# Attention in 64-token steps of two batches, in 64x64 quarters of the array, with transposed outputs

## The chip, the cores and the metric

The kernel runs on one NeuronCore of a Trainium2 chip. The metric is the device time of one execution in microseconds. Engine names are those of the profile: PE is the matrix engine (PEld its weight loads), DVE the vector engine, ACT the scalar engine, POOL the GpSimd engine, SP the engine that issues most DMAs here.

## The reference

The reference is a gated linear attention followed by a feed-forward layer. With 4 batches, 8 heads, 768 tokens and a head size of 48:

```python
for t in range(S):
    state = alpha[:, :, t, :, None] * state + np.einsum('bhd,bhe->bhde', k[:, :, t], v[:, :, t])
    y[:, :, t] = np.einsum('bhd,bhde->bhe', q[:, :, t], state)
x = y.transpose(0, 2, 1, 3).reshape(B * S, H * D)        # 3072 x 384
h = x @ w_in                                             # 384 -> 2048
sp = np.maximum(h, 0.0) + np.log1p(np.exp(-np.abs(h)))
out = (h * erf(sp)) @ w_out                              # 2048 -> 384
```

## The kernel before

Attention goes in 24 chunks of 128 tokens of one batch, six in a row for each batch. The steps of a chunk are methods of `Chunk`:

- `ld` issues seven DMAs on SP's queue (alpha, k and q in two halves each, v once) into one set of raw tiles. Heads go in pairs: partitions 0 to 47 hold the dimensions of the even head of a pair, 64 to 111 those of the odd one, with the 128 tokens along the free axis. `a0` counts entries of alpha above a limit.
- `a1` forms the running product A of alpha along the tokens, one scan of 128 elements for each of the four pairs.
- `a2` and `a3` form 1/A (by Ln, Exp and a correction step on DVE), the scaled keys K = k/A and the scaled queries Q = q*A.
- `a4` multiplies K and Q of each head to the 128x128 scores pS, masks them into sT (one DVE operation for the even heads, one for the odd ones), and transposes K to pn, copied to kn.
- `a5` forms the outputs py, with tokens on the partitions: Q times the state T, plus masked scores times v. They are copied to y by ACT. Then pu = kn times v updates the state T (four DVE operations on 64 partitions each; in the first chunk of a batch two).
- `a6` transposes y on PE (px) and splits it into two float32r parts, x_hi (ACT) and x_lo (DVE), each 384 columns for the chunk.

Two chunks make a block of 256 tokens, whose feed-forward layer is `Moe`. `H` multiplies x by w_in (tile ph; three products for each pair of parts, f32r, 144 matmuls of 256 columns a block), `L1`, `L2`, `E` and `Z` are the activation on ACT and DVE, and `O` multiplies by w_out (tile acc, 96 matmuls of 384 columns a block).

The order in which steps are given out is written by hand in the tables `START`, `ORDER` and `TAIL`; within it a scheduler orders each engine's instructions. `START` also loads and splits the weights, `ORDER` is repeated for the blocks in between. `a5_0` there is the second chunk of the next block, `a5_1` the first of the one after that:

```python
"... Z_2@-1 ld_1 a5_0 a6_0 H_0_0@1 H_0_1@1 L2_0 L2_1 O_2_0@-1 O_2_1@-1 "
"O_3_0@-1 L1_2 L2_2 a1_1 a2_1 a3_1 a4_1 O_3_1@-1 L1_3 L2_3 a5_1 a6_1 ld_2 out@-1 "
```

If values leave the range that this way can carry, `general` computes everything anew; with these inputs it does not run.

Of the kernel before, what the change touches and what calls it, by code (L numbers as in the profile page):

```python
# [14 lines left out]
AMIN = 1e-18  # L15
# [5 lines left out]
AHI = 1.3  # L21
# [5 lines left out]
# The order in which the steps of chunks (128 tokens) and blocks (256) are given out: the start with the weights, the  # L27
# same for each block in between, and the end.
# [21 lines left out]
def gla_moe(ctx: ExitStack, tc: tile.TileContext, q, k, v, alpha, w_in, w_out, out):  # L50
    nc = tc.nc
    B, CPB, _, D, NP, P = q.shape
    H, S = 2 * NP, CPB * P
# [25 lines left out]
    for nm, fill in (("a", 1.0), ("q", 0.0), ("k", 0.0)):  # L79
        t = raw.tile([P, NP, P], F32, name=f"raw_{nm}")  # L80
        nc.vector.memset(t, fill)
        raws.append(t)
# [3 lines left out]
    maskn = const.tile([P, P], F32, name="maskn")  # L86
    nc.gpsimd.memset(maskn, -1.0)
    nc.gpsimd.affine_select(
        out=maskn, in_=maskn, pattern=[[1, P]], compare_op=ALU.is_ge, fill=0.0, base=0, channel_multiplier=-1
    )  # L90
# [4 lines left out]
    flags = const.tile([P, B * CPB, 2], F32, name="flags")  # L95
# [3 lines left out]
    nc.gpsimd.memset(hflags, 0.0)  # L99

# [20 lines left out]
    state = {"T": at.tile([P, NP, 2, D], F32, name="T", tag="T", bufs=1)}  # L121
    nc.gpsimd.memset(state["T"], 0.0)

    class Chunk:
        def __init__(self, n):
            self.n = n
            self.first = n % CPB == 0
            self.last = n % CPB == CPB - 1

        def ld(self):  # L130
            b, c = divmod(self.n, CPB)
            self.ra, self.rq, self.rk = raws
            self.vt = raw.tile([P, H, D], F32, name="raw_v", tag="raw_v")
            for t, src in ((self.ra, alpha), (self.rk, k), (self.rq, q)):
                for par in range(2):
                    nc.sync.dma_start(out=t[par * HD : par * HD + D], in_=src[b, c, par])
            nc.sync.dma_start(out=self.vt, in_=v[b, c])

        def a0(self):
            junk = at.tile([P, NP, P], F32, name="junk", tag="w", bufs=1)  # L140
            nc.scalar.activation(junk, self.ra, AF.Relu, bias=bhi, accum_out=flags[:, self.n, 1:2])

        def a1(self):
            self.A = at.tile([P, NP, P], F32, name="A", tag="A", bufs=1)
            for pair in range(NP):
                nc.vector.tensor_tensor_scan(  # L146
                    out=self.A[:, pair, :], data0=self.ra[:, pair, :], data1=floor.broadcast_to([P, P]), initial=1.0,
                    op0=ALU.mult, op1=ALU.max,
                )
            self.ae = at.tile([P, NP], F32, name="ae", tag="ae")  # L150
            nc.gpsimd.tensor_copy(out=self.ae, in_=self.A[:, :, P - 1])

        def a2(self):
            r = ps_at.tile([P, NP, P], F32, name="r", tag="at")
            tab(nc.scalar.activation(r, self.A, AF.Ln))
            tab(nc.scalar.activation(r, r, AF.Exp, scale=-1.0, accum_out=flags[:, self.n, 0:1]))
            w = at.tile([P, NP, P], F32, name="w", tag="w", bufs=1)
            nc.vector.tensor_tensor(out=w, in0=self.A, in1=r, op=ALU.mult)
            nc.vector.scalar_tensor_tensor(out=w, in0=w, scalar=2.0, in1=r, op0=ALU.subtract, op1=ALU.mult)
            self.w = w  # L160

        def a3(self):
            self.K = at.tile([P, NP, P], F32, name="K", tag="K")
            nc.vector.tensor_tensor(out=self.K, in0=self.rk, in1=self.w, op=ALU.mult)
            self.Q = at.tile([P, NP, P], F32, name="Q", tag="Q")
            nc.vector.tensor_tensor(out=self.Q, in0=self.rq, in1=self.A, op=ALU.mult)

        def a4(self):
            self.sT = []
            pss = [ps_at.tile([P, NP, P], F32, name="pS", tag="at") for _ in range(2)]  # L170
            for pair in range(NP):
                for par in range(2):
                    rows = slice(par * HD, par * HD + D)
                    nc.tensor.matmul(  # L174
                        out=pss[par][:, pair, :], lhsT=self.K[rows, pair, :], rhs=self.Q[rows, pair, :],
                        start=True, stop=True,
                    )
            for ps in pss:
                st = at.tile([P, NP, P], F32, name="sT", tag="sT")
                nc.vector.tensor_tensor(  # L180
                    out=st, in0=ps, in1=maskn.unsqueeze(1).broadcast_to([P, NP, P]), op=ALU.mult
                )
                self.sT.append(st)
            if not self.last:
                pn = ps_at.tile([P, NP, P], F32, name="pn", tag="at")
                for pair in range(NP):
                    nc.tensor.transpose(pn[:, pair, :], self.K[:, pair, :], ident)  # L187
                self.kn = at.tile([P, NP, 2, HD], F32, name="kn", tag="kn", bufs=1)
                nc.scalar.activation(
                    self.kn.rearrange("p a b d -> p (a b d)"), pn.rearrange("p a t -> p (a t)"), AF.Copy  # L190
                )

        def a5(self):
            vt, T = self.vt, state["T"]
            self.yt = at.tile([P, NP, 2, D], F32, name="y", tag="y", bufs=1)
            py = ps_at.tile([P, 512], F32, name="py", tag="at")
            for pair in range(NP):
                if not self.first:
                    nc.tensor.matmul(  # L199
                        out=py[:, 2 * pair * D : 2 * (pair + 1) * D], lhsT=self.Q[:, pair, :],  # L200
                        rhs=T[:, pair, :, :].rearrange("p b d -> p (b d)"), start=True, stop=False,
                    )
                for par in range(2):
                    h = 2 * pair + par
                    nc.tensor.matmul(  # L205
                        out=py[:, h * D : (h + 1) * D], lhsT=self.sT[par][:, pair, :], rhs=vt[:, h, :],
                        start=self.first, stop=self.first or par == 1,
                    )
            nc.scalar.activation(self.yt.rearrange("p a b d -> p (a b d)"), py[:, : H * D], AF.Copy)
            if not self.last:  # L210
                pu = ps_at.tile([P, 512], F32, name="pu", tag="at")
                for pair in range(NP):
                    for par in range(2):
                        nc.tensor.matmul(  # L214
                            out=pu[par * HD : (par + 1) * HD, pair * D : (pair + 1) * D],
                            lhsT=self.kn[:, pair, par, :], rhs=vt[:, 2 * pair + par, :], start=True, stop=True,
                        )
                U = pu[:, : NP * D].rearrange("p (a d) -> p a d", a=NP)
                aeb = self.ae.unsqueeze(2).broadcast_to([P, NP, D])
                for par in range(2):  # L220
                    rows = slice(par * HD, (par + 1) * HD)
                    Tp, Up, ap = T[rows, :, par, :], U[rows], aeb[rows]
                    if self.first:
                        nc.vector.scalar_tensor_tensor(
                            out=Tp, in0=Up, scalar=-1.0, in1=ap, op0=ALU.mult, op1=ALU.mult
                        )
                    else:
                        nc.vector.tensor_tensor(out=Tp, in0=Tp, in1=Up, op=ALU.subtract)
                        nc.vector.tensor_tensor(out=Tp, in0=Tp, in1=ap, op=ALU.mult)

        def a6(self, moe):
            if self.n % 2 == 0:
                moe.alloc_x()
            moe.turn(self.yt.rearrange("p a b d -> p (a b d)"), self.n % 2, ps_at, "at")
# [3 lines left out]
    class Moe:  # L238
        def __init__(self, tok, pl):
            self.tok, self.pl = tok, pl  # L240
# [6 lines left out]

        def turn(self, y, c, pool, tag):
            """Writes the 128 tokens of y, transposed, to the block's x as two parts."""
            x_hi, x_lo = self.x  # L250
            cs = slice(c * P, (c + 1) * P)
            px = pool.tile([P, 512], F32, name="px", tag=tag)
# [6 lines left out]
        def H(self, g, half):  # L259
# [21 lines left out]
            else:  # L281
                n = (self.tok // TB * NG + g) * 2 + half
# [53 lines left out]
        def out(self):  # L336
            for tt in range(2):
                o = self.pl.gp.tile([P, DM], F32, name="o", tag="o", bufs=1)
                nc.scalar.activation(o, self.acc[tt][:, :DM], AF.Copy, scale=-RT2)
                nc.sync.dma_start(out=out[bass.ds(self.tok + tt * P, P), :], in_=o)  # L340
# [5 lines left out]
    def weight(hi, lo, src, n, pool, tag):  # L346
        """Loads a matrix of float32, or of float64 as pairs of int32, and splits it into two parts."""
# [195 lines left out]
```

## Time and profile before

| what | value |
|---|---|
| runs (three) | 597.25, 598.33, 598.65 us; median 598.33 |
| profiled execution, span from first to last instruction | 594.3 us |
| PE busy | 552.4 us (93%) |
| DVE busy | 503.0 us (85%) |
| ACT busy | 485.1 us (82%) |
| POOL busy | 20.9 us (4%) |
| DMA | 36.98 MB, mean 62 GB/s |
| mean granted PE clock | 0.984 of full speed |

For the profiled execution the profile gives the span alone; the time of a run is taken around it. Matmuls are pipelined, so the records of PE overlap, and a busy PE is not a PE at its peak. The chain of waits, followed back from the last instruction, is PE for 81% of the span, DVE for 9% and ACT for 6%.

### The profile page before, as it was taken

The page shows a single profiled execution, that of the slowest core. Times are in us where ns is not written, and L with a number is a line of the kernel's source. Part 1 is how long each engine was busy: PE and PEld are TensorE (multiplying, and loading weights), DVE is VectorE, ACT ScalarE, POOL GpSimd, SP SyncE. Part 2 cuts the span into 40 slices and gives each one's busy share as a digit, 9 for nine tenths or more (in the row PEclk, how much of TensorE's full clock was granted, in tenths as well). Part 3 has the DMA queues.
Part 4 walks back from the last instruction along what each step waited for, and adds up shares of the span by engine and source line. Part 5 has one row for each costly group of instructions (what it writes and reads, how often), then busy time and mean ns, then how long its engine had stood idle before and what let it go on. Part 6 is the DMA issues. An engine that isn't in the chain of part 4 may idle for free.

```text
span 594.3 us, 11033 instructions
## 1 busy us (share of the span) xinstructions
PE 552.4 (93%) x4282; PEld 534.8 (90%) x4282; DVE 503.0 (85%) x769; ACT 485.1 (82%) x845; POOL 20.9 (4%) x40
## 2 busy tenths in 40 slices
PE   0679798999999999999999999999999999999994
PEld 0568787999999999999999999999999999999884
DVE  7899999999999869869779879879779879758780
ACT  4558979698989879889879879889788888889941
POOL 1000110002000000000000000000000000000000
PEclk9999798998999999999999999999999999999998
DMA  6584312313112102112112102112112101000001
GB/s 196 176 290 145 110 55 81 120 54 94 28 41 81 41 26 68 41 29 68 40 28 68 41 28 67 41 39 70 28 35 66 34 28 41 1 1 28 1 27 33
DMA packets 20220, 36.98 MB, mean 62 GB/s; under 512 B 3520, under 2 KB 9664, under 8 KB 20160
## 3 DMA queue, kind: packets, MB, share of 16 engines
q1 hardware_dynamic: 20160, 36.19, 19.9%
q8 instruction: 36, 0.59, 0.4%
q14 instruction: 24, 0.20, 0.1%
HBM read 31.46 MB, written 4.72 MB: 61 GB/s over the span
## 4 chain that ended last, share of the span: by engine, by line
PE 81%; DVE 9%; ACT 6%; DMA 2%; issue 1%; SPq 0%; ACTq 0%; DVEq 0%
PE acc L331 33%; PE ph L272 30%; PE py L205 7%; PE pS L174 4%; PE py L199 3%; PE pu L214 2%; DMA wst<-in_moe_w_in_dram 2%; PE pn L187 1%; PE px L254 1%; DVE hs L309 1%; DVE s L308 1%; DVE A L146 1%; ACT wbuf L360 1%; ACT w L283 1%; DVE wbuf L365 1%
## 5 line engine op out<-in xcount | busy, mean ns | idle before, releaser
L272 PE MATMUL ph<-x_hi,wi_hi 128*128 128x256 f32 x576 | 164.0, 288 | 4.0 <-ACT hs L284 3.4
L272 PE MATMUL ph<-x_lo,wi_hi 128*128 128x256 f32 x576 | 163.4, 284 | 0.4 <-DVE x_lo L257 0.4
L272 PE MATMUL ph<-x_hi,wi_lo 128*128 128x256 f32 x576 | 163.2, 284 | 0.0
L331 PE MATMUL acc<-wo_hi,gh 128*128 128x384 f32 x384 | 134.5, 351 | 3.6 <-DVE gh L320 2.6
L331 PE MATMUL acc<-wo_lo,gh 128*128 128x384 f32 x384 | 131.3, 342 | 0.0
L331 PE MATMUL acc<-wo_hi,gl 128*128 128x384 f32 x384 | 130.0, 344 | 1.2 <-DVE gl L323 1.2
L272 PEld LDWEIGHTS ph<-x_hi,wi_hi 128*128 128x128 f32 x576 | 110.4, 192 | 5.8 <-ACT hs L284 4.2
L272 PEld LDWEIGHTS ph<-x_lo,wi_hi 128*128 128x128 f32 x576 | 110.5, 192 | 0.7 <-DVE x_lo L257 0.7
L272 PEld LDWEIGHTS ph<-x_hi,wi_lo 128*128 128x128 f32 x576 | 110.5, 192 | 0.5 <-DVE wi_lo L344 0.5
L283 ACT ACTIVATE w<-ph 128x512 f32<-128x512 f32 x96 | 57.5, 599 | 46.9 <-PE ph L272 44.0
L297 DVE TENSOR_TENSOR t<-s,w 128x1024 f32<-128x1024 f32 x48 | 58.5, 1219 | 29.4 <-ACT w L291 29.3
L331 PEld LDWEIGHTS acc<-wo_hi,gh 128*128 128x128 f32 x384 | 72.8, 190 | 5.3 <-DVE gh L320 2.6
L331 PEld LDWEIGHTS acc<-wo_hi,gl 128*128 128x128 f32 x384 | 72.2, 190 | 2.6 <-DVE gl L323 2.6
L323 DVE TENSOR_TENSOR gl<-hs,gh 128x512 fp32r<-128x512 f32 x96 | 65.3, 683 | 10.8 <-ACT gh L322 10.3
L331 PEld LDWEIGHTS acc<-wo_lo,gh 128*128 128x128 f32 x384 | 73.2, 191 | 0.0
L205 PE MATMUL py<-raw_v,sT 128*128 128x48 f32 x384 | 57.9, 279 | 5.5 <-DVE sT L180 5.5
L308 DVE TENSOR_TENSOR s<-s,w 128x1024 f32<-128x1024 f32 x48 | 58.2, 1218 | 2.3 <-ACT s L303 2.1
L205 PEld LDWEIGHTS py<-raw_v,sT 128*128 128x128 f32 x384 | 53.8, 203 | 6.8 <-DVE sT L180 6.6
L298 DVE SCALAR_TENSOR_TENSOR w<-t,w 128x1024 f32<-128x1024 f32 x48 | 58.4, 1217 | 0.4
L309 DVE SCALAR_TENSOR_TENSOR hs<-s,hs 128x1024 f32<-128x1024 f32 x48 | 58.2, 1217 | 0.3
L289 ACT ACTIVATE s<-w,fixed 128x1024 f32<-128x1024 f32 x48 | 55.1, 1151 | 0.0
L284 ACT ACTIVATE hs<-ph 128x512 f32<-128x512 f32 x96 | 54.8, 593 | 0.0
(67 smaller groups left out, 834.2 us busy)
## 6 DMA issues: line engine op xcount, KB each, us to landing
wst<-in_moe_w_in_dram SPq DMA_DIRECT2D x12, 512.0 KB, 4.6
wst<-in_moe_w_out_dram SPq DMA_DIRECT2D x16, 384.0 KB, 3.4
raw_a<-in_alpha_dram SPq DMA_DIRECT2D x48, 96.0 KB, 2.2
raw_k<-in_k_dram SPq DMA_DIRECT2D x48, 96.0 KB, 2.2
raw_q<-in_q_dram SPq DMA_DIRECT2D x48, 96.0 KB, 2.2
raw_v<-in_v_dram SPq DMA_DIRECT2D x24, 192.0 KB, 2.4
out_dram<-o SPq DMA_DIRECT2D x24, 192.0 KB, 1.9
```

The lines of the kernel that those rows point to most:

```text
L174: nc.tensor.matmul(out=pss[par][:, pair, :], lhsT=self.K[rows, pair, :], rhs=self.Q[rows, pair, :], start=True, stop=True,)
L205: nc.tensor.matmul(out=py[:, h * D : (h + 1) * D], lhsT=self.sT[par][:, pair, :], rhs=vt[:, h, :], start=self.first, stop=self.first or pa ...
L272: nc.tensor.matmul(out=o, lhsT=wt[:, kt, fs], rhs=xt[:, kt, :], start=n == 0, stop=n == 3 * KT - 1)
L283: tab(nc.scalar.activation(w, ph, AF.Exp, accum_out=self.pl.flags[:, n : n + 1]))
L284: nc.scalar.activation(self.hs[g][:, sl], ph, AF.Copy)
L289: tab(nc.scalar.activation(s, w, AF.Ln, bias=bone))
L297: nc.vector.tensor_tensor(out=t, in0=s, in1=w, op=ALU.mult)
L298: nc.vector.scalar_tensor_tensor(out=w, in0=t, scalar=2.0, in1=w, op0=ALU.subtract, op1=ALU.mult)
L308: nc.vector.tensor_tensor(out=s, in0=s, in1=w, op=ALU.mult)
L309: nc.vector.scalar_tensor_tensor(out=h, in0=s, scalar=RT2 / 2, in1=h, op0=ALU.add, op1=ALU.mult)
L323: nc.vector.tensor_tensor(out=gl.rearrange("p a t -> p (a t)"), in0=gg, in1=ghf.bitcast(F32), op=ALU.subtract)
L331: nc.tensor.matmul(out=self.acc[tt][:, :DM], lhsT=gt[:, u, ts], rhs=wt[:, f, :], start=f == 0 and n == 0, stop=f == NF - 1 and n == 2,)
```

## The change

A step now takes 64 tokens of two batches instead of 128 tokens of one: still 128 tokens a step and 24 steps, but two sequences of twelve. All matmuls of attention but the transposes of K have 64 rows or fewer and 64 columns, and address a 64x64 quarter of the array: scores and outputs the two quarters on the diagonal, the state's update all four. Even heads use partitions 0 to 63 and odd heads 64 to 127 of their outputs, which share a bank. py now has the output's dimensions on the partitions and the tokens along the free axis, so px and its transposes go; instead the fourth pair's 48 rows are moved by six DMAs a block, 16 rows each, into rows 48 to 63 and 112 to 127 of the other three pairs' tiles, and the rows of w_in are put in the same order ahead of the launch. v is loaded a second time (vx), with the pairs split by parity, in four DMAs of 192-byte pieces. Raw tiles come in two sets. The four scans become one of 512, which restarts where a POOL operation has put a zero in alpha and the first value into the lower bound. The count on alpha becomes one on A.

```diff
-    for nm, fill in (("a", 1.0), ("q", 0.0), ("k", 0.0)):
-        t = raw.tile([P, NP, P], F32, name=f"raw_{nm}")
-        nc.vector.memset(t, fill)
+    for n in range(2):
+        ra, rq, rk = (raw.tile([P, NP, NI, TC], F32, name=f"raw_{nm}{n}") for nm in "aqk")
+        rv = raw.tile([P, H * D], F32, name=f"raw_v{n}")
+        rx = raw.tile([P, NI * NP * D + HD - D], F32, name=f"raw_x{n}")
+        for t, fill in ((ra, 1.0), (rq, 0.0), (rk, 0.0), (rx, 0.0)):
+            (nc.vector if n == 0 else nc.gpsimd).memset(t, fill)
...
         def ld(self):
+            nc.sync.dma_start(out=self.vt, in_=v[self.m, self.c])
+            for par in range(2):
+                for i in range(NI):
+                    nc.sync.dma_start(out=self.vx[par * HD : (par + 1) * HD, ...], in_=v[...][:, par])
         def a1(self):
-            for pair in range(NP):
-                nc.vector.tensor_tensor_scan(
-                    out=self.A[:, pair, :], data0=self.ra[:, pair, :], data1=floor.broadcast_to([P, P]), initial=1.0,
+            nc.gpsimd.tensor_scalar(
+                out=lower[:, :, :, 0], in0=first, scalar1=AMIN, scalar2=None, op0=ALU.max
+            )
+            nc.gpsimd.memset(first, 0.0)
+            nc.vector.tensor_tensor_scan(
+                out=self.A.rearrange(flat), data0=self.ra.rearrange(flat), data1=lower.rearrange(flat), initial=1.0,
         def a2(self):
-            r = ps_at.tile([P, NP, P], F32, name="r", tag="at")
+            r = at.tile([P, W], F32, name="r", tag="r", bufs=1)
+            nc.scalar.activation(r, A, AF.Relu, bias=bhi, accum_out=flags[:, self.n, 1:2])
         def a4(self):
-            pss = [ps_at.tile([P, NP, P], F32, name="pS", tag="at") for _ in range(2)]
+            ps = ps_at.tile([P, NP * NI, TC], F32, name="pS", tag="at")
             for pair in range(NP):
-                for par in range(2):
-                    rows = slice(par * HD, par * HD + D)
-                    nc.tensor.matmul(
-                        out=pss[par][:, pair, :], lhsT=self.K[rows, pair, :], rhs=self.Q[rows, pair, :],
+                for i in range(NI):
+                    for par in range(2):
+                        rows = slice(par * HD, par * HD + D)
+                        nc.tensor.matmul(
+                            out=ps[par * HD : (par + 1) * HD, pair * NI + i, :],
+                            lhsT=K[rows, pair, i, :], rhs=Q[rows, pair, i, :], start=True, stop=True,
...
         def a5(self, moe):
+            for pair in range(NP):
+                for i in range(NI):
+                    at0 = (i * NP + pair) * D
+                    for par in range(2):
+                        o = py[par * HD : (par + 1) * HD, pair * NI + i, :]
+                        if not self.first:
+                            nc.tensor.matmul(
+                                out=o, lhsT=T[par * HD : par * HD + D, at0 : at0 + HD],
+                                rhs=self.Q[par * HD : par * HD + D, pair, i, :], start=True, stop=False,
+                            )
+                        nc.tensor.matmul(
+                            out=o, lhsT=vx[par * HD : (par + 1) * HD, at0 : at0 + HD],
+                            rhs=self.sT[par * HD : (par + 1) * HD, pair * NI + i, :], start=self.first, stop=True,
+                        )
...
+                        for i in range(NI):
+                            toks, h = slice(i * TC, (i + 1) * TC), 2 * pair + par
+                            nc.tensor.matmul(
+                                out=pu[i][par * HD : (par + 1) * HD, pair * D : (pair + 1) * D],
+                                lhsT=self.kn[toks, pair, par, :], rhs=vt[toks, h * D : (h + 1) * D],
+            nc.scalar.activation(moe.xf[:, :, :, s, :].rearrange("p a i t -> p (a i) t"), py, AF.Copy)
...
         def a6(self, moe):
-            moe.turn(self.yt.rearrange("p a b d -> p (a b d)"), self.n % 2, ps_at, "at")
+            for j in range(KT):
+                for par in range(2):
+                    nc.sync.dma_start(
+                        out=xf[par * HD + D : (par + 1) * HD, j, :],
+                        in_=xf[par * HD + j * G : par * HD + (j + 1) * G, NP - 1, :],
+                    )
+            moe.alloc_x()
+            nc.scalar.activation(x_hi, xf[:, :KT, :], AF.Copy)
+            nc.vector.tensor_tensor(out=x_lo, in0=xf[:, :KT, :], in1=x_hi.bitcast(F32), op=ALU.subtract)
...
-    nc = _bacc.Bacc("TRN2", target_bir_lowering=False, num_devices=1)
+    nc = _bacc.Bacc("TRN2", target_bir_lowering=False, num_devices=1, dynamic_dma_scratch_size=2048)
...
+        elif name == "moe_w_in":
+            a = a[order]
```

Where the work stands in the engines' rows, the diff does not tell. On PE, the second chunk of a block in the repeated part, from its outputs to the next block's first layer. Before (names are output<-inputs, with the tile's shape and a count):

```order
L205 MATMUL py<-raw_v,sT 128x48 x2
L214 MATMUL pu<-raw_v,kn 64x48 x8
L331 MATMUL acc<-wo_hi,gh 128x384
L331 MATMUL acc<-wo_lo,gh 128x384
L254 MATMUL px<-ident,y 128x128 x3
L331 MATMUL acc<-wo_hi,gl 128x384
...
L272 MATMUL ph<-x_hi,wi_hi 128x256 x2
```

Now:

```order
L239 MATMUL py<-sT,raw_x_104 64x64
L249 MATMUL pu<-raw_v_103,kn 64x48 x16
L393 MATMUL acc<-wo_hi,gh 128x384
...
L204 MATMUL pn<-ident,K 128x128
L334 MATMUL ph<-x_hi,wi_hi 128x256 x2
L204 MATMUL pn<-ident,K 128x128 x3
L215 MATMUL pS<-Q,K 64x64 x9
L334 MATMUL ph<-x_lo,wi_hi 128x256
```

The transposes px are gone. Before, 8 acc matmuls stood between pu and the first ph; now 36 acc and one pn do, and the next step's pS is cut by the block's ph matmuls (its other 7 stand 34 ph later).

On SP, the same place, from the loads of one step past those of the next. Before:

```order
L340 DMA out_dram<-o 128x384
L136 DMA raw_k<-in_k_dram 48x512 x2
L136 DMA raw_a<-in_alpha_dram 48x512 x2
L136 DMA raw_q<-in_q_dram 48x512 x2
L137 DMA raw_v<-in_v_dram 128x384
```

Now:

```order
L402 DMA out_dram<-o 128x384
L149 DMA raw_k_102<-in_k_dram 48x512 x2
L149 DMA raw_a_91<-in_alpha_dram 48x512 x2
L149 DMA raw_q_92<-in_q_dram 48x512 x2
L154 DMA raw_x_104<-in_v_dram 64x4x48 x3
L278 DMA xf<-xf 16x256 x6
L151 DMA raw_v_103<-in_v_dram 128x384
```

The six moves of xf stand behind three loads of raw_x (in other blocks behind one or two), which all wait for the same py.

On DVE, the first step of the start. Before:

```order
L146 SCALAR_TENSOR_TENSOR A<-raw_a,fixed 128x128 x4
L344 TENSOR_TENSOR wo_lo<-wbuf,wo_hi 128x384
L166 TENSOR_TENSOR Q<-raw_q,A 128x512
L158 TENSOR_TENSOR w<-A,r 128x512
L159 SCALAR_TENSOR_TENSOR w<-w,r 128x512
L164 TENSOR_TENSOR K<-raw_k,w 128x512
```

Now:

```order
L406 TENSOR_TENSOR wo_lo<-wbuf,wo_hi 128x384
L171 SCALAR_TENSOR_TENSOR A<-raw_a_91,lower 128x512
L195 TENSOR_TENSOR Q<-raw_q_92,A 128x512
L187 TENSOR_TENSOR K<-A,r 128x512
L188 SCALAR_TENSOR_TENSOR K<-K,r 128x512
L193 TENSOR_TENSOR K<-raw_k_93,K 128x512
```

The four scans are one, of four times the length, and the rest keeps its shape.

More of the change, by code (lines that the diff above doesn't have):

```diff
@@ L126, in __init__ @@
             self.n = n
-            self.first = n % CPB == 0
-            self.last = n % CPB == CPB - 1
+            self.m, self.c = divmod(n, CPB)
+            self.first = self.c == 0
+            self.last = self.c == CPB - 1
         def ld(self):
-            b, c = divmod(self.n, CPB)
-            self.ra, self.rq, self.rk = raws
-            self.vt = raw.tile([P, H, D], F32, name="raw_v", tag="raw_v")
+            self.ra, self.rq, self.rk, self.vt, self.vx = raws[self.n % 2]
             for t, src in ((self.ra, alpha), (self.rk, k), (self.rq, q)):
@@ L193, in a5 @@
[L193 to L211, printed above, removed]
+                    nc.sync.dma_start(out=t[par * HD : par * HD + D], in_=src[self.m, self.c, par])
@@ L212, in a5 @@
                 for pair in range(NP):
                     for par in range(2):
[L214 to L222, printed above, removed]
+                        for i in range(NI):
+                            toks, h = slice(i * TC, (i + 1) * TC), 2 * pair + par
+                            nc.tensor.matmul(
+                                out=pu[i][par * HD : (par + 1) * HD, pair * D : (pair + 1) * D],
+                                lhsT=self.kn[toks, pair, par, :], rhs=vt[toks, h * D : (h + 1) * D],
+                                start=True, stop=True,
+                            )
@@ L223, in a5 @@
+            nc.scalar.activation(
+                moe.xf[:, :, :, s, :].rearrange("p a i t -> p (a i) t"), py, AF.Copy,
+            )
+            if not self.last:
+                aeb = self.ae.unsqueeze(3).broadcast_to([P, NI, NP, D])
+                for i in range(NI):
+                    U = pu[i][:, : NP * D].rearrange("p (a d) -> p a d", a=NP)
                     if self.first:
                         nc.vector.scalar_tensor_tensor(
-                            out=Tp, in0=Up, scalar=-1.0, in1=ap, op0=ALU.mult, op1=ALU.mult
+                            out=Tv[:, i], in0=U, scalar=-1.0, in1=aeb[:, i], op0=ALU.mult, op1=ALU.mult
@@ L246, in alloc_x, with order @@
             self.x = (x_hi, x_lo)
+        def order(self, y):
+            t = self.pl.gp.tile([P, KT, 2, HD], F32, name="yo", tag="yo", bufs=1)
+            pairs = y.rearrange("p (a b d) -> p a b d", a=NP, b=2)
+            nc.vector.tensor_copy(out=t[:, :, :, :D], in_=pairs[:, :KT])
+            for j in range(KT):
+                G = HD - D
+                nc.vector.tensor_copy(out=t[:, j, :, D:], in_=pairs[:, NP - 1, :, j * G : (j + 1) * G])
+            return t.rearrange("p j b d -> p (j b d)")
         def turn(self, y, c, pool, tag):
@@ L452, in gla_moe @@
     new_phase(LNEXP)
[L454 to L455 removed]
+    chunks = [Chunk(n) for n in range(NS)]
+    moes = []
+    for n in range(NBLK):
+        m, j = divmod(n, CPB // 2)
+        moes.append(Moe(n, [(m * NI + i) * S + j * P for i in range(NI)], pools))
     def run(order, c0, b0):
```

183 lines of the change are left out of this document (108 added, 75 removed).

## Prediction

> **What bounds the kernel now.** I read the page's busy shares, then the table by stages, then the waits of TensorE, then the chain of waits around one attention step, and last the groups by form.
>
> ```profile
> span 594.3 us, 11033 instructions
> PE 552.4 (93%) x4282; PEld 534.8 (90%) x4282; DVE 503.0 (85%) x769; ACT 485.1 (82%) x845; POOL 20.9 (4%) x40
> ```
>
> The profiled span is 594.3 us; the median of the runs is 598.33, so 4.0 us lie outside the span. I make the sum against the span and add 4.0. Runs differ by 1.4 us, so a change under 0.3% (1.8 us) can't be told from none.
>
> ```profile
> 0.00:135.00 135.00, 103.69 (x765) 96.83 (x766) 127.19 (x238) 103.02 (x197) 10.54 (x23) 0.96 0.44 136
> 265.47:310.01 44.54, 44.54 (x364) 43.63 (x363) 37.76 (x54) 38.28 (x67) 1.36 (x2) 1.00 0.16 47
> 310.01:354.80 44.79, 44.79 (x368) 43.88 (x368) 38.02 (x57) 38.13 (x67) 0.83 (x2) 1.00 0.15 46
> PE py L205 <- DVE sT L180: 0.6, 1, 0.6
> ```
>
> The columns are stretch, length, then busy us of PE, weight loads, DVE, ACT and POOL. Two regimes: in the start (0 to 135 us, with the weights being split) DVE is busy 127.2 of 135 us and PE 103.7. In a steady block of 256 tokens PE is busy without a gap (44.54 of 44.54, 44.79 of 44.79), with DVE at 38.0 and ACT at 38.3 us. The last row is all that PE waited for from 142.8 to 528 us. So PE time saved in a steady block is time saved, until ACT's 38 us is met; in the start, DVE time counts.
>
> ```profile
> 312.63 1.09 PE pS L174 x16
> 313.73 0.59 PE pn L187 x4
> 314.31 2.12 PE acc L331 x12
> 316.43 0.20 PE py L199 x2
> 316.62 0.45 PE py L205 x4
> ...
> 319.08 0.60 PE pu L214 x16
> ...
> 320.41 0.33 PE px L254 x3
> ```
>
> This is the chain over one chunk (start, us, what). From 316.43 to 319.08 py takes 2.65. Attention on PE is 1.09 + 0.59 + 2.65 + 0.60 + 0.33 = 5.26 us a chunk. An acc matmul is 2.12 / 12 = 0.177.
>
> **The change, part by part.** *Matmuls.* A step still handles 128 tokens, so there are still 24. pS goes from 16 to 32 records, py from 24 to 64, pu from 16 to 32 (each f32 matmul leaves two records), all with 64 weight columns; pn stays; px goes. What decides is the price of a record in a quarter, which nothing shows. The nearest rows:
>
> ```profile
> 312.56 1.16 PE L174 MATMUL pS<-Q,K 48*128 48x128 f32 x16
> 319.01 0.67 PE L214 MATMUL pu<-raw_v,kn 128*64 128x48 f32 x16
> L174 PE MATMUL pS<-Q,K x384: 272/272/579, 15.2 to 510.9; 48*128 48x128 f32 x192
> L214 PE MATMUL pu<-raw_v,kn x320: 222/222/343, 23.1 to 496.6; 128*64 128x48 f32 x160
> ```
>
> The first two give start and length of a run of 16 records, the others min, median and max of one. Two halves of the array work at once here: less the last record, pu spends 0.67 - 0.22 = 0.45 us on seven steps of two records, 0.064 us a step; pS 1.16 - 0.27 = 0.89, or 0.127. One py record alone takes about 0.45 / 4 = 0.11 with 128 columns, so the two row halves of pS do run side by side, and so do the two column halves of pu. Half the columns, half the time. I price a slot, in which each quarter in use does one record, at 0.064, the row with 64 columns. Changing the array's shape costs what is left of the chain rows: 1.09 - 0.89 = 0.20 for pS, 0.60 - 0.45 = 0.15 for pu.
>
> After: pS uses the two diagonal quarters, 32 records, 15 steps: 0.96 + 0.20 = 1.16. py uses the same two and pu all four, with no change of shape between: 32 + 8 slots, 39 steps: 2.50 + 0.15 = 2.65. pn 0.59. Sum 4.40, against 5.26: 0.86 less a step. If pu's quarters only go two at a time it is 8 slots, 0.51, more. In the first step of a sequence the T part is missing on both sides (0.20 and three more pieces of 0.26 before, 0.98; 16 slots, 1.02, after): 0.90. In the last, without pn and pu: 4.07 before, 1.16 + 0.15 + 1.98 = 3.29 after: 0.78. After the start there are 14 full steps, one first and two last: 12.0 + 0.9 + 1.6 = 14.5 us.
>
> The order takes some back: in most blocks pS of one step is cut by the next block's first-layer matmuls (pS x9, ph, pS x7), ten cuts after the start, each one more change of shape and back: 10 x 0.20 = 2.0. Steady: 14.5 - 2.0 = 12.5.
>
> One rule of the Trainium skill speaks against this. Its page "TensorEngine Tiling (Array Packing)", section "Restrictions and Gotchas", says that different row tiles cannot access the same PSUM bank simultaneously. Now pS and py send both row halves to one bank, if to separate partitions; in the rows above pS had a bank for each half, and only pu's column halves shared one. By the rule the two lanes would take turns and the time be that of the rival "in turns" below; by the rows it is 0.064 a slot, which I take, as the halves never meet in a partition.
>
> *DVE.* One scan of 512 for four of 128, one masking for two, three T operations over 128 rows for four over 64, one x_lo of 768 for two of 384 in a block, one memset more.
>
> ```profile
> L146 DVE TENSOR_TENSOR_SCAN A<-raw_a,fixed 128x128 f32<-128x128 f32 x96 | 35.1, 406 | 0.0
> L180 DVE TENSOR_TENSOR sT<-pS,maskn 128x512 f32<-128x512 f32 x48 | 30.9, 679 | 0.4 <-PE pS L174 0.4
> L166 DVE TENSOR_TENSOR Q<-raw_q,A 128x512 f32<-128x512 f32 x24 | 16.5, 687 | 0.4
> L257 DVE TENSOR_TENSOR x_lo<-px,x_hi 128x384 fp32r<-128x384 f32 x24 | 13.4, 557 | 11.3 <-ACT x_hi L256 10.5
> L229 DVE TENSOR_TENSOR T<-T,ae 64x192 f32<-64x192 f32 x32 | 11.3, 353 | 0.8
> L228 DVE TENSOR_TENSOR T<-T,pu 64x192 f32<-64x192 f32 x32 | 11.2, 351 | 10.0 <-PE pu L214 9.1 <-PE py L199 0.4
> L81 DVE MEMSET raw_a<- 128x512 f32 x1 | 0.5, 485 | 1.0 <-PEq L519 1.0
> ```
>
> From 384 to 512 elements an operation goes from 557 to 687 ns: 1.02 ns an element, 0.17 us fixed. A scan of 512 then takes 0.17 + 4 x (0.406 - 0.17) = 1.11; the ends are 0.69 (the plain operation of that size) and 1.62 (no gain). I take 1.11: 0.51 less. Masking: 0.68 less. T: 2 x 0.35 + 0.56 for 1.41: 0.15 less. x_lo: 0.95 for 1.11, 0.08 a step. That is 1.4 us a step. The start has seven scans, six maskings, four full T updates, three blocks of x_lo: 3.6 + 4.1 + 0.6 + 0.5 - 0.5 = 8.3 us. It is bounded by 0 and 8.3. I let 5 appear, 0.5 less for each of the seven scans, since the POOL hop below (1.6 us) stands ahead of a scan on an engine with no slack. In the steady part DVE's saving lies beside PE and counts nothing.
>
> *The way of x.* Before: y copied, three transposes, x_hi, x_lo. Now py is already transposed; xf is copied, six DMAs on SP's queue move 16 rows each, then x_hi and x_lo for the whole block.
>
> ```profile
> 311.35 0.78 SPq L136 DMA_DIRECT2D raw_a<-in_alpha_dram  x2
> 312.22 1.30 SPq L136 DMA_DIRECT2D raw_q<-in_q_dram  x2
> DMA to landing us min/median/max: 2.0/2.2/5.3
> L189 ACT ACTIVATE kn<-pn 128x512 f32<-128x512 f32 x20 | 11.8, 591 | 1.1 <-PE pn L187 1.1
> L209 ACT ACTIVATE y<-py 128x384 f32<-128x384 f32 x24 | 11.8, 490 | 14.3 <-PE py L205 14.3
> L290 ACT ACTIVATE w<-s 128x1024 f32<-128x1024 f32 x48 | 50.8, 1058 | 0.1
> ```
>
> Two issues take 0.78 to 1.30 us, 0.4 each as a rule. In SP's queue up to three loads of raw_x, freed by the same py, stand ahead of the six: the ninth issue starts 8 x 0.4 = 3.2 us after py and lands 2.2 later (the landing row is raw_a's). The xf copy (0.59, as kn) lies beside the first loads. x_hi of 768 is 0.83, between 0.59 for 512 and 1.06 for 1024. In all 3.2 + 2.2 + 0.83 = 6.2, with 0.1 for semaphores 6.3 us from py to the first ph. PE has meanwhile pu (0.51), 36 acc (6.37) and a pn: 7.0. So the hop is covered with 0.7 us to spare, and I cost it at 0; with a landing of 5.3 PE waits 2.4 us a block. x_lo comes 0.95 later, behind two ph, three pn and half of pS. Kn and the exponentials stand behind x_hi on ACT; ACT has 6 us a block free.
>
> ACT else: Relu moves behind the scan at the same size, xf costs 0.1 more than y, x_hi 0.15 less a block. Nothing.
>
> *POOL and loads.* Every scan now waits for two small POOL operations.
>
> ```profile
> L151 POOL COPY ae<-A 128x4 f32<-128x4 f32 x24 | 19.1, 797 | 467.6 <-DVE A L146 467.6
> q1 hardware_dynamic: 20160, 36.19, 19.9%
> ```
>
> A POOL copy of 4 elements takes 0.8 us, so two are 1.6 ahead of a scan; with two sets of raw tiles the load arrives a step early, which hides it in the steady part. Four more loads a step, in pieces of 192 bytes, are 1.6 us of SP, idle there. All DMA goes through the hardware's queue, so the smaller descriptor scratch does nothing. New row order of w_in, mask, flags and the general path: nothing timed.
>
> Sum: 594.3 - 12.5 - 5 + 4.0 = 580.8; I forecast **581**. With the ends of the open prices (8.3 for 5; cuts free; pu in two lanes, 15 x 0.51 = 7.7; 0 for 5) the likeliest case spans 575.5 to 593.5; its own range is 574 to 594.
>
> **The rivals.**
> *Late x (slower).* The hop becomes PE's wait. It decides when the hop exceeds 7.0 us by (12.5 + 5) / 9 blocks = 1.9 us, a hop of 8.9. Landings of 5.3 give 2.4 x 9 = 21.6 us: 602. For it: nine issues in one burst, and the 5.3. Against: the median is 2.2, and these DMAs stay small.
> *In program order.* If a quarter can start a record only after all earlier ones started, py's groups (four records on one quarter, then four on the other) overlap by one record: 49 slots for 32, 17 x 0.064 = 1.1 us a step, over 17 steps 18.5: 599. Rows can't exclude it: pS and pu alternate after two records. The Trainium skill's "TensorE: Matmul & The Clock Gate", Part 3, says matmuls start and end in program order, which would be this case.
> *In turns.* The diagonal quarters alternate, since both write one bank (no row shows row halves doing that): pS 31 steps, py and pu 71: 2.18 + 4.69 + 0.59 = 7.46, 2.2 us more than before, 37 in 17 steps, plus 2.0 for the cuts, less the start's 5: 632.
> *Hidden.* PE shrinks, but ACT and DVE, at 38 of 44.5 us with waits between them, don't follow: only the start's 5 and a third of the 12.5 appear: 589.
>
> **How the numbers follow.** Likeliest 0.66 (574 to 594); hidden 0.11 (586 to 598, faster but for 0.02); in program order 0.07 (597 to 603); late x 0.10 (597 to 610); in turns 0.06. Faster: 0.66 + 0.09 = 0.75, and 0.01 from late x. Same: 0.02 + 0.03 + 0.01 = 0.06. Slower: 0.18. The range 571 to 603 leaves out in turns, half of late x and little below.
>
> **What would show it.** Right: 16 pu records within some 0.5 us and all py within 2.1; a steady block of 42.5 to 43.5 us with PE still without gaps; 12 to 15 us less from 142.8 to 528; DVE still near full in the start, which ends about 5 us sooner; no PE wait for x_hi. Wrong: ph waiting for x_hi or its DMA (late x), py near 3.2 us (program order) or 4.2 (in turns), PE gaps that end with ACT (hidden), or idle DVE in the start ahead of a scan (POOL).

## The result, and the profile after

The changed kernel takes 12250.55 us (median of 4 runs, 12246.0 to 12255.16); the kernel before took 597.79 beside it. The ratio is 20.53 (95% interval 20.47 to 20.59). The forecast was 581.

Two things happened, of very different size. First the page of the changed kernel, then its table by stretches (columns as before: stretch, length, PE, weight loads, DVE, ACT, POOL, granted clock, DMA share, GB/s).

```profile
span 12244.2 us, 71388 instructions
PE 1118.9 (9%) x8866; PEld 1056.0 (9%) x8866; DVE 3834.0 (31%) x4999; ACT 1174.3 (10%) x1627; POOL 63.7 (1%) x94
...
L478 DVE TENSOR_TENSOR st<-st,ga 128x576 f32<-128x576 f32 x768 | 575.1, 749 | 7289.3 <-DMA gk<-in_k_dram 6675.3
...
ga<-in_alpha_dram SPq DMA_DIRECT2D x4608, 1.0 KB
```

```profile
0.00:135.00 135.00, 86.16 (x1077) 80.00 (x1078) 112.45 (x192) 92.53 (x169) 23.29 (x45) 0.85 0.53 153
284.16:328.47 44.31, 42.74 (x471) 40.64 (x471) 34.47 (x44) 37.88 (x66) 7.04 (x6) 1.00 0.21 57
328.47:373.81 45.34, 44.23 (x507) 42.32 (x507) 35.84 (x46) 38.22 (x65) 3.59 (x6) 1.00 0.21 56
611.00:11164.00 10553.00, 0.00 (x0) 0.00 (x0) 2979.66 (x3840) 0.00 (x0) 0.00 (x0) 0.50 0.03 5
11164.00:12244.00 1080.00, 574.67 (x2952) 537.58 (x2952) 374.66 (x504) 687.35 (x792) 0.00 (x0) 0.74 0.07 22
```

From 611 us on, the tiles are st, ga, gk: `general()`, the token-by-token path, runs. Its recurrence takes 10553 us, in which VectorE works 2980 and mostly waits for loads of 1 KB, 4608 each of alpha, k and q (6675 us for k alone); then the layers are computed once more, 1080 us.

Ahead of that the fast part is slower too. Its last output copy is at 610.4 us, before at 588.7. The first copy is at 150.3, before at 135.65: 14.7 us of the 21.7 are lost by the end of the first block. In the middle, from the third copy to the 21st (nine blocks), it is 393.5 us for 383.5, 43.7 a block for 42.6. PE now has gaps (42.74 of 44.31, 44.23 of 45.34), where before it had none.

The waits of the middle (142.8 to 556 us; who waits for what, us in total, times, longest):

```profile
PE acc L393 <- DVE gl L385: 4.0, 6, 0.8
PE ph L334 <- ACT x_hi L284: 3.2, 4, 1.4
...
ACT w L345 <- PE ph L334: 39.2, 24, 3.4
ACT x_hi L284 <- DMA xf<-xf: 17.1, 9, 3.2
```

PE's own named waits are small. ACT waits longest for PE's ph, as it did before (40.9 us). The new long wait is at x_hi: nine times ACT stands there for the DMAs of xf, and what is queued on ACT behind x_hi comes later.

### The profile page after: what moved, and what is told of

Same layout as the page of the kernel before. It is cut to its first block, busy times and chain, and to the rows that moved or that the text cites. A ratio compares the mean times of both kernels' runs of the same rounds, so it can differ in the third digit from the quotient of the medians.

```text
span 12244.2 us, 71388 instructions
## 1 busy us (share of the span) xinstructions
PE 1118.9 (9%) x8866; PEld 1056.0 (9%) x8866; DVE 3834.0 (31%) x4999; ACT 1174.3 (10%) x1627; POOL 63.7 (1%) x94
## 5 line engine op out<-in xcount | busy, mean ns | idle before, releaser
L478 DVE TENSOR_TENSOR st<-st,ga 128x576 f32<-128x576 f32 x768 | 575.1, 749 | 7289.3 <-DMA gk<-in_k_dram 6675.3
L481 DVE TENSOR_REDUCE gy<-kv 128x48 f32<-128x576 f32 x768 | 856.9, 1116 | 26.7
L477 DVE TENSOR_TENSOR kv<-gk,gv 128x576 f32<-128x576 f32 x768 | 575.8, 751 | 149.5 <-DMA gv<-in_v_dram 149.5
L480 DVE TENSOR_TENSOR kv<-st,gq 128x576 f32<-128x576 f32 x768 | 582.0, 758 | 26.4
L479 DVE TENSOR_TENSOR st<-st,kv 128x576 f32<-128x576 f32 x768 | 576.8, 751 | 0.4
L334 PE MATMUL ph<-x_hi,wi_hi 128*128 128x256 f32 x1152 | 355.0, 310 | 174.2 <-ACT hs L346 164.0
L334 PE MATMUL ph<-x_lo,wi_hi 128*128 128x256 f32 x1152 | 349.2, 304 | 1.5 <-DVE x_lo L285 1.4
L334 PE MATMUL ph<-x_hi,wi_lo 128*128 128x256 f32 x1152 | 343.8, 299 | 0.0
L393 PE MATMUL acc<-wo_hi,gh 128*128 128x384 f32 x768 | 302.4, 394 | 186.9 <-ACT gh L384 104.7
L393 PE MATMUL acc<-wo_lo,gh 128*128 128x384 f32 x768 | 291.8, 380 | 0.3 <-DVE wo_lo L406 0.3
```

The source lines that it names most:

```text
L334: nc.tensor.matmul(out=o, lhsT=wt[:, kt, fs], rhs=xt[:, kt, :], start=n == 0, stop=n == 3 * KT - 1)
L393: nc.tensor.matmul(out=self.acc[tt][:, :DM], lhsT=gt[:, u, ts], rhs=wt[:, f, :], start=f == 0 and n == 0, stop=f == NF - 1 and n == 2,)
L477: nc.vector.tensor_tensor(out=kv, in0=wide(gk), in1=vb, op=ALU.mult)
L478: nc.vector.tensor_tensor(out=st, in0=st, in1=wide(ga), op=ALU.mult)
L479: nc.vector.tensor_tensor(out=st, in0=st, in1=kv, op=ALU.add)
L480: nc.vector.tensor_tensor(out=kv, in0=st, in1=wide(gq), op=ALU.mult)
```

## The experiments

In `START`, which the change left as it was, `ld_5` stands ahead of `a5_3`. Before, each load of v took a new tile; now v and raw_x lie in the two fixed raw sets, chunks 3 and 5 both use set 1, and chunk 3 is computed with chunk 5's values in the fast part (in the changed kernel the long path then writes all outputs anew). The kernels of the first two groups, and e_vxact and e_xfpool, keep that; all others have `a5_3 ld_5` and compute everything. No run changes this order alone, but it does hold chunk 3 up. In e_rmax (start, us, what):

```profile
80.06 2.51 SPq L154 DMA_DIRECT2D raw_x<-in_v_dram  x4
80.37 0.42 PE L235 MATMUL py<-Q,T 48*64 48x64 f32 x2
85.15 0.23 PE L239 MATMUL py<-sT,raw_x 64*64 64x64 f32 x1
```

The first product of chunk 3's py starts at 80.37 us, the first that reads raw_x at 85.15, behind the loads for chunk 5. In e_vq, with `a5_3 ld_5`, py's first product is at 76.83 and the rest run from 78.49 without a break. So what a run with the old order says of raw_x in the start holds some of this too.

All times are medians in us; the ratio is to the kernel before, run on the same chip. "First copy" and "block" (mean of nine middle blocks) are read from the profiled execution; two executions of the same instructions differ by some 2 us in the first (150.3 and 148.5 for after and e_rmax) and 0.2 in the second. The chips differ as well (the kernel before took 596.1 beside e_rmax, 597.8 beside e_both, 596.2 beside e_vq), so between groups the ratios are the better comparison.

| run | time | ratio, 95% interval | first copy | block |
|---|---|---|---|---|
| before | 595.5 to 597.8 | 1 | 135.65 | 42.61 |
| e_pad | 619.17 | 1.0372 [1.0337, 1.0407] | 152.1 | 43.87 |
| e_rmax | 619.02 | 1.0379 [1.0349, 1.0409] | 148.5 | 43.93 |
| e_noxf | 601.74 | 1.0090 [1.0060, 1.0120] | 142.6 | 42.40 |
| e_novx | 604.39 | 1.0138 [1.0106, 1.0171] | 139.6 | 43.47 |
| e_both | 591.35 | 0.9901 [0.9877, 0.9925] | 136.8 | 42.35 |
| e_vxact | 613.47 | 1.0258 [1.0231, 1.0285] | 147.7 | 43.57 |
| e_xfpool | 620.09 | 1.0390 [1.0350, 1.0430] | 151.1 | 43.74 |
| e_vqp | 611.18 | 1.0231 [1.0201, 1.0260] | 140.5 | 43.90 |
| e_vq | 609.10 | 1.0216 [1.0194, 1.0238] | 140.1 | 43.57 |
| e_cover | 596.61 | 1.0005 [0.9985, 1.0025] | 142.5 | 42.19 |
| e_dve | 606.90 | 1.0185 [1.0162, 1.0209] | 138.4 | 43.57 |
| e_cdvep | 594.42 | 0.9968 [0.9949, 0.9987] | 139.4 | 41.88 |
| e_relu | 594.92 | 0.9984 [0.9962, 1.0006] | 139.1 | 41.90 |
| e_ps2r | 613.44 | 1.0275 [1.0237, 1.0313] | 139.9 | 43.77 |
| e_rsplit | 594.65 | 0.9966 [0.9943, 0.9988] | 141.7 | 41.86 |

**Why the long path runs.** e_pad:

```
-            nc.gpsimd.memset(first, 0.0)
+            for par in range(2):
+                nc.gpsimd.memset(self.ra[par * HD : par * HD + D, :, :, 0], 0.0)
```

> The changed kernel, but a chunk's first products are set to zero only on the rows that hold data (0 to 47 and 64 to 111), by two POOL operations for one. Theory 'padding rows': in the changed kernel the zero also falls on the rows 48 to 63 and 112 to 127, which no load fills again; at the second use of a raw set the bound there is 1e-18, its inverse 1e18 is over RMAX (1e17), the flag goes up and the token-by-token path runs. Then this kernel ends near 616 us of span, about 620 us (last output copy of the fast part at 610.4 in the changed kernel, and the 9.6 us that the kernel before has between that copy, 588.7, and its whole time). Rival 'another flag' (the gain or an exponential): it stays at 12250 us. Rival 'as predicted once the path is out': 581 us.

e_rmax changes one number, `RMAX = 1e30` for 1e17:

> The changed kernel with one number changed: RMAX 1e30 for 1e17, so that the sum of inverse products can't raise its flag; every instruction of the fast part stays. Padding rows (512 x 1e18 = 5e20): the path is not run and the time is that of the fast part as the changed kernel has it, 618 to 621 us, 3 to 4% slower than before. If the gain flag or an exponential's raises it: 12250 us.

Both take 619 us, as the theory of the padding rows has it; "another flag" and "as predicted once the path is out" fall. `a1` sets `first`, column 0 of raw_a, to zero on all 128 rows. `ld` fills 96 of them again; rows 48 to 63 and 112 to 127 were filled with 1.0 once, ahead of everything. At a raw set's second use they hold 0 there, `lower` becomes 1e-18, the scan carries 1e-18 through the row, and the sum of its inverses is 512 x 1e18, over 1e17. The flag counts every row, the padding too.

**What the added DMAs cost the fast part.** Three kernels on e_rmax: e_noxf without the loop of six DMAs in `a6`, e_novx without the four loads of raw_x in `ld` (`for i in range(0)`), e_both without either.

> As the run with RMAX 1e30, and the six DMAs of each block inside SBUF (rows 48 to 63 of xf) left out; 16 rows of each half of x then hold other heads' values. Theory 'x hop': the hop costs what x_hi waits for these DMAs, 2 us a block in the middle and some 4 us in the start: 600 to 608 us. Rival 'hidden': PE waits for other things, 617 to 621 us.

> As the run with RMAX 1e30, and the four loads of raw_x of each chunk left out (raw_x stays zero, so y lacks the part within a chunk). Theory 'full queue': these loads take 4 x 0.64 us of SP's queue in each of the start's eight chunks, 20 us, and the weights' loads stand behind them; without them the start is 8 to 14 us shorter: 606 to 612 us. Rival 'queue idle', as the prediction had it: 617 to 621 us.

> RMAX 1e30, and both kinds of added DMA left out: the six inside SBUF of each block and the four loads of raw_x of each chunk (y then lacks the part within a chunk, and 16 rows of each half of x hold other heads' values). Theory 'the added DMAs are all of it': the two savings measured alone, 17.3 and 14.6 us, overlap only where both free the same queue, and what is left is the prediction without a hop, 581 to 590 us. Rival 'one cause in two places' (either of them alone frees the start's queue, the second adds little): 597 to 601 us.

Against e_rmax the six DMAs of a block cost 17.3 us, the loads of raw_x 14.6, both 27.7 (28.5 by the ratios, as e_both ran on another chip); "hidden" and "queue idle" fall. They cost in different places: the six take 6 us of the start and 13.8 of the nine middle blocks (some 3 us of it go back, 1 between the first and the third copy and 2 in the tail), raw_x takes 9 of the start, in part by the order above, and 4.1 of the middle. Without both the kernel is just under the one before, 1 us over the upper end of what was expected.

This is the chain of waits of e_rmax around one block's x (start, us, what), with rows of the same hop left out:

```profile
353.92 1.32 PE ph L334 x11
355.25 0.27 PE py L235 x4
...
357.19 0.05 PE pu L249 x2
357.24 0.01 PE py L239 x2
357.25 0.54 PE pu L249 x22
357.79 1.53 SPq L154
359.32 0.05 issue
359.38 0.60 SPq L154
...
360.07 0.57 SPq L278
360.64 0.05 issue
360.69 0.58 SPq L278
...
362.58 0.59 SPq L278
363.17 0.04 issue
363.21 1.78 DMA xf<-xf
364.99 0.02 issue
365.01 0.04 ACTq L284
365.05 0.04 issue
365.10 0.85 ACT x_hi L284
365.95 0.04 issue
365.99 0.51 PE ph L334 x2
```

From the last py to the first ph 8.75 us: raw_x issues ahead (one of them took 1.64 us, the longest of the row below; what made it long the trace does not show), six issues of xf at 0.63 each from one to the next, 1.8 to land, 0.85 for x_hi. Over the nine middle blocks it is 7.3 to 9.6, 8.5 as a mean, where PE has 7.0 us of other work: 1.5 us a block, 13.5 in nine, close to the 13.8 that e_noxf gives back (2.5 of these are pS and pn, which the late x cuts in pieces in e_rmax and which run whole in e_noxf). The lengths of the issues and of x_hi, from the groups by tile of e_rmax (ns min/median/max):

```profile
L154 SPq DMA_DIRECT2D raw_x<-in_v_dram x96: 538/588/1639, 7.6 to 500.5; - x96
...
L278 SPq DMA_DIRECT2D xf<-xf x72: 507/587/1194, 32.9 to 543.3; - x72
...
L284 ACT ACTIVATE x_hi<-xf x12: 827/844/862, 45.9 to 545.2; 128x768 fp32r<-128x768 f32 x12
```

**Queue, or length of the hop?** e_vxact issues raw_x by `nc.scalar`, e_xfpool the six by `nc.gpsimd`, both on e_rmax. e_vqp is complete: zeros as in e_pad, `a5_3 ld_5`, v in DRAM with the heads of a pair apart and two loads of raw_x a chunk, xf by `nc.gpsimd`; e_vq is e_vqp with xf by `nc.sync`.

```
+                nc.sync.dma_start(
+                    out=self.vx[par * HD : (par + 1) * HD, : NI * NP * D].rearrange("t (i x) -> t i x", i=NI),
+                    in_=v[self.m, self.c].rearrange("(i t) (b x) -> b t i x", i=NI, b=2)[par],
+                )
```

> RMAX 1e30, and the four loads of raw_x of each chunk issued from ScalarE's queue instead of SyncE's; the same pieces of 192 bytes move. Theory 'issue time on SP's queue': most of the 14.6 us that leaving them out gave comes back, less what ScalarE pays for issuing: 604 to 611 us. Rival 'the small pieces load the DMA engines': 617 to 621 us, no better than from SyncE. Rival 'ScalarE has no room in the start': over 621 us.

> RMAX 1e30, and the six DMAs inside SBUF of each block issued from GpSimd's queue instead of SyncE's. Theory 'in order behind raw_x on SP': without the loads ahead of them x_hi comes earlier and weights' loads no longer stand behind them: 605 to 612 us. Rival 'the hop itself' (issue and landing, whatever the queue): 615 to 621 us. GpSimd's own issue is not in any trace yet; if one takes 1 us and more, six of them delay the bounds of the next scan: over 621 us.

> All of the computation, with four edits: the first products set to zero on the data rows alone; ld_5 behind a5_3 in START (in the changed kernel's order chunk 5's values are loaded over chunk 3's before a5_3 reads them); v laid out in DRAM with the two heads of a pair apart, so that raw_x takes two loads of 128 pieces of 768 bytes a chunk for four of 256 pieces in all of 192; and the six DMAs of xf from GpSimd's queue. Theory 'queue': SP is relieved of 2 x 0.64 us a chunk and 6 x 0.6 us a block: 598 to 606 us. Rival 'the hop itself and the POOL steps ahead of the scan': 610 to 618 us.

> The run 'e_vqp' with the six DMAs of xf back on SyncE's queue: all of the computation, zeros on the data rows alone, ld_5 behind a5_3, v laid out so that raw_x takes two loads a chunk. Theory 'hop by its length, not by its queue': the same as from GpSimd's queue, 608 to 613 us (start to the first output copy 139 to 143 us, a middle block 43.8 us). Rival 'SP is the bottleneck': 614 to 618 us.

For xf the queue doesn't matter: from GpSimd 620 for 619, and e_vqp and e_vq have overlapping intervals. An issue is 0.48 us there for 0.59, but a DMA then takes 2.3 us to land for 1.8 (medians), and the hop stays: x_hi starts 7.0 us after the last py on average (5.7 to 8.4), 7.6 from SyncE. That the hop stayed is the likely reason why e_vqp missed its 598 to 606. For raw_x, another queue gives some 6 of the 14.6 us back (7 by the ratios; less than expected). From e_pad to e_vq, with half as many issues in larger pieces, the time falls by about 10, nearly all in the start; but e_vq also has `a5_3 ld_5`, and no run parts the two.

**Cover for the hop, and the steps ahead of the scan.** e_cover is e_vq with the DMAs of xf moved to the end of `a5` and the middle order changed:

```
-"Z_3@-1 O_1_1@-1 H_3_1 L1_0 L1_1 Z_2@-1 ld_1 a5_0 a6_0 H_0_0@1 H_0_1@1 L2_0 L2_1 O_2_0@-1 O_2_1@-1 "
+"a5_0 Z_3@-1 O_1_1@-1 H_3_1 L1_0 L1_1 Z_2@-1 ld_1 L2_0 L2_1 O_2_0@-1 O_2_1@-1 a6_0 H_0_0@1 H_0_1@1 "
```

e_dve is e_vqp with the two small operations of `a1` on `nc.vector`, and `floor` (1.0 on the padding rows) as the bound; e_cdvep has both edits and xf by GpSimd.

> As 'e_vq', and the order of the middle blocks changed: a5_0 (with the DMAs of xf at its end) stands ahead of O_1_1 and H_3_1 of the block before, and H_0_0@1 behind O_2_0 and O_2_1. PE then has between the last py of a block and its first ph: pu, 36 acc and 18 ph, 0.5 + 6.4 + 2.15 = 9.0 us for 7.0, and pS isn't cut. Theory 'the uncovered hop': last py to first ph is 8.2 to 10.4 us in the run with RMAX 1e30 and 4.1 less without the DMAs, where a middle block was 42.4 us; with the cover a block goes from 43.9 to 42.4 to 43.0 us, the time to 596 to 604 us. Rival 'ScalarE and VectorE are what the block waits for': 43.9 a block, the time that of 'e_vq'.

> As 'e_vqp', but the two small operations ahead of each scan on VectorE in place of GpSimd, with the bound of the padding rows held at 1.0 by a column of constants (so no second zeroing). Theory 'POOL hop': in the start the scan waits for GpSimd (0.8 to 1.6 us each time, seven times): 603 to 607 us, all of it ahead of the first output copy. Rival 'the hop is hidden behind the loads': 609 to 613 us; two operations more on VectorE, 0.3 us a chunk, cost up to 2 us in the start.

> The three edits together: the order of 'e_cover', the small operations of the scan on VectorE, the DMAs of xf from GpSimd's queue. If both theories hold, a middle block of 42.4 to 43.0 us and a start of 135 to 138 us: 592 to 599 us, within 1% of before. If neither: 610 us.

With the same DMAs and the same hop (x_hi 7.0 to 7.8 us after py) e_cover's block goes from 43.57 to 42.19 us and the time from 609.1 to 596.6: PE has other work meanwhile. "ScalarE and VectorE are what the block waits for" falls. The new order also leaves pS in one piece; pS and pn take 23.0 us in the nine blocks for 25.2 in e_vq, which is 0.24 of the 1.38 us a block. That the rest is the hop is borne out by e_noxf, which has the old order, no hop, pS whole as well, and 42.40 a block. e_dve is 4 us under e_vqp, 2.7 by the ratios, since the two ran on different chips; the intervals overlap a little (1.0201 and 1.0209) and 2 us are ahead of the first copy, so a gain is likely, not shown. e_cdvep is the first that computes everything and beats the kernel before, by 0.3%.

**Is PE still the bound, and where is the start's gain?** e_relu is e_cdvep with the Relu of `a2` moved behind the products of K and Q in `a3`; e_ps2r is e_relu with each matmul of pS issued twice (`for par in (0, 1, 0, 1)`); e_rsplit is e_relu with three DMAs of xf by GpSimd and three by SyncE.

> As 'e_cdvep', and the Relu that watches for a gain, which the change put between the scan and the logarithm on ScalarE, moved behind the products of K and Q. Theory 'the Relu delays K': its 0.72 us and the read of its sum (0.19, 0.22 apart) stand in the chain scan, Ln, Exp, K, on which TensorE waits in the start (24.4 us for K); 0.8 us in each of the first chunks, 1.5 to 4 us of the start: 590 to 593 us. Rival 'hidden' (the start is bound by VectorE's total): 594 to 595 us, the time of 'e_cdvep'.

> As 'e_relu', with every matmul of pS issued twice (the second writes the same values again): 32 records more a chunk, 0.96 us by the slot of 0.03 us a record, 1.9 us a block. Theory 'TensorE still bounds a middle block': 41.9 becomes 43.7 to 43.9 us, the time rises by 22 to 25 us (24 chunks). Rival 'ScalarE, VectorE and the chain through the table loads bound it': under 0.8 us a block, under 10 us in all.

> As 'e_relu', with three of the six DMAs of xf issued by GpSimd and three by SyncE, at the same time. Theory: the hop is some 1.4 us shorter; in the middle it is covered already (x_hi ends 2.9 us ahead of its first matmul), so only the start's three blocks can gain: 0 to 3 us less than 'e_relu'. Rival: SyncE has loads ahead of its three and the hop grows: 1 to 5 us more.

The nine middle blocks of e_cdvep, and then of e_ps2r (same columns):

```profile
187.06:563.98 376.92, 371.31 (x4098) 360.53 (x4098) 305.80 (x406) 331.27 (x557) 46.02 (x62) 1.00 0.16 47
```

```profile
190.06:584.00 393.94, 386.38 (x4579) 373.99 (x4578) 307.87 (x405) 332.53 (x559) 34.65 (x62) 1.00 0.15 45
```

The doubled pS adds 1.87 us to a block: PE, at 371 of 377 us, is what bounds a covered block. That 1.9 was expected is in part luck, as it counted two steps a block, and the nine blocks hold 15: pS itself grew by 14.0 us, 1.56 a block, and PE's idle time by 0.24. The whole time rose less than expected (18.5, not 22 to 25), as part of it is hidden in the start. Of the 20.7 us between the profiled executions 0.8 lie ahead of the first copy, 3.4 between it and the third, and 16.9 in the nine blocks. e_relu shows no difference from e_cdvep: the Relu's place costs nothing that can be measured, my theory falls. e_rsplit neither gains nor loses.

## Why the prediction was wrong, step by step

**"New row order of w_in, mask, flags and the general path: nothing timed."** This is the step that failed, by 11630 us, as e_pad and e_rmax show. That the long path stays off was taken from the run before. But the change moved the scan's first column into data: a zero is written into a tile of which a quarter is never loaded again, and a flag looks at all of it. No duration in the profile could tell; reading who writes rows 48 to 63 after their first use could.

**Matmuls: right.** The same nine blocks hold 15 steps of attention. From start to start their matmuls took 73.7 us before and 61.3 in e_cdvep, 12.4 less, 0.83 a step; the prediction had 0.86. (Its 12.5 is for 17 steps, less 2.0 for the cuts of pS. e_cdvep has no cuts; e_rmax has them, and its pS and pn take 25.5 us in the nine blocks for 23.0.) py takes 1.94 us for its 64 records (355.25 to 357.19 in the chain above), 0.030 a record. The chain also shows that two quarters work at once, both writing one bank: four records of T (L235, two matmuls) alternate with four of sT (L239), though `a5` gives T and sT of one quarter and then T and sT of the other, so the second quarter starts ahead of the first one's last. That refutes "in turns" (4.2 us), so the rule of the Trainium skill's "TensorEngine Tiling (Array Packing)", "Restrictions and Gotchas", on row tiles and one bank is not what this trace shows for separate partitions. "In program order" (3.2 us) falls as well: what the Trainium skill's "TensorE: Matmul & The Clock Gate", Part 3, says of starts in program order doesn't keep these two lanes from overlapping. Pu took 0.6 to 0.7 us, in four lanes, as taken.

Of these 12.4 us the nine blocks of e_cdvep give back 6.5 (383.5 to 376.9). PE's busy time fell by 10.3 (381.6 to 371.3), and its idle time grew by 3.7, most of it a wait that before did not have, for ACT's copies of the output (187.06 to 563.98 us):

```profile
PE acc L392 <- ACT o L400: 3.5, 8, 0.8
```

So a part of the rival "hidden" is there as well.

**The way of x, costed at 0: wrong, and the rival "late x" was the case.** The mechanism and its threshold were as written there (cover 7.0); the size was off. The term that was mis-sized is "the ninth issue starts 8 x 0.4 = 3.2 after py": in the chain above it starts 6.0 after (363.21 for 357.24). An issue of these shapes is 0.59, not 0.4 as for a raw_a load, and one in front of them took 1.64. The landing was shorter than priced (1.8 for 2.2), x_hi right (0.84 for 0.83). The hop is 8.5, not 6.3, and costs 1.5 us a block and 6 in the start, less the 3 that go back: 17.3 together. The prediction looked for it as a PE wait on x_hi; most of it appears as ACT waiting in its own queue, and PE then waits in small pieces for gl, x_hi and gh.

**"Four more loads a step ... are 1.6 us of SP, idle there": wrong in the start.** They take 4 x 0.59 = 2.4 us, and in the changed kernel SP issues from 8 to 30 us with two pauses alone, of 1.0 and 2.6 us, weights behind raw_x. 9 of the 14.6 us are lost ahead of the first copy; how much of that is the queue and how much chunk 3's wait for chunk 5's raw_x stays open.

**The start's 5 us: none appeared.** Even e_both, free of the added DMAs, has its first copy at 136.8 for 135.65; its profiled execution was 4 us above its median, though, so that figure may be late by some of that. The scans' saving was mis-sized on both sides: the scan of 512 took 1.218 us (24 of them, 1.21 to 1.225), between the ends given, not 1.11, and four scans of 128 kept DVE busy for 1.46, not 1.62 (35.1 us for 96 in the prediction's own row, as their records overlap). A scan so saves 0.24, not 0.51. This is e_both's row for the first 135 us:

```profile
0.00:135.00 135.00, 95.38 (x1182) 89.42 (x1183) 123.25 (x210) 104.38 (x192) 25.33 (x43) 0.92 0.45 143
```

DVE's busy time in it fell from 127.2 to 123.3. By operation, the scans went from 10.2 to 8.5 us, the maskings from 7.9 to 4.1, x_lo from 3.3 to 2.8; T rose from 6.3 to 6.6, as chunk 5 is no longer the last of a sequence, and a memset took 0.4. So some 5.3 of the 8.3 are there as work, and DVE idles instead: 11.8 us for 7.8. So "in the start, DVE time counts" did not hold for these. Its waits for ACT's r are 2.7 us for 1.1 before, but e_relu, which shortens that way, gained nothing. With the small operations on DVE the start gained 2 us at most. What else holds it is open; the granted clock there is lower (0.85 in the changed kernel, 0.92 in e_both, 0.96 before), which goes with an emptier PE but isn't shown to be the cause.

The sum for the fast part: without the added DMAs the kernel is 1.0% under the one before (e_both), with them 3.8% over it (e_rmax), so by the ratios the DMAs add 28.5 us. What e_cdvep's profiled span (592.6 us) lacks to the forecast (594.3 - 17.5 = 576.8) is the start, 139.4 for 130.7, nine blocks of 41.9 for 41.2, and 2.3 us in the tail, less 1.4 between the first copy and the third. The 4.0 us that the prediction added for what lies outside the span are too much: in the later runs a time is 1.7 to 2.3 us above its own span, and the profiled execution of the kernel before was a faster one than the median.

## What to carry to other kernels

When a change replaces a pass by writing into its input tile, list for every row and column of that tile who writes it next; a guard that reduces over padding turns a stale cell into a second kernel, and a path that computes everything anew hides a fault of the fast one, here chunk 3's values. Price an added DMA by its own shape, and its hop from the last producer to the first consumer with all that its queue holds ahead of it, then compare that with the work that the order really puts between the two; where the cover is short by one or two us, moving the producer forward is worth more than another queue. A kernel with one full engine in the middle and another in the start has two sums: time saved on the first can be lost by a queue that is idle only in the middle.

## What the runs showed of the hardware that I had not expected

An f32 matmul with 64 weight columns and 64 moving columns on 48 or 64 rows costs a diagonal quarter 0.06 us a record with two quarters at work, though both write the same bank. A DMA's issue differs with its shape: as a rule 0.31 to 0.42 us for 48 rows of 2 KB, 0.59 for 256 pieces of 192 bytes and as much for 16 rows of 1 KB from SBUF to SBUF, 0.48 for these from GpSimd (first row, e_xfpool); single issues from SyncE took up to 2.1 (raw_x in e_noxf). And small operations on GpSimd vary widely, as far as the profile's spans there, which are rough, can tell: in e_rmax the copy of 128x8 elements to ae took between 0.19 and 4.7 us (24 of them, second row), on VectorE the operation of the same size for the bound, in e_cdvep, 0.22 to 0.23 (third row).

```profile
L278 POOL DMA_DIRECT2D xf<-xf x72: 484/484/705, 34.1 to 544.4; - x72
```

```profile
L176 POOL COPY ae<-A x24: 191/1376/4727, 12.8 to 497.7; 128x8 f32<-128x8 f32 x24
```

```profile
L162 DVE TENSOR_SCALAR lower<-raw_a,fixed x24: 220/226/229, 11.5 to 464.5; 128x8 f32<-128x8 f32 x24
```
